# Mixing three weight tiles in every attention unit instead of three and two in turn, in a fused linear attention and spectral mixing kernel

## The chip, the cores and the metric

The kernel runs on one core of one Trainium2 chip. The metric is device time in microseconds (us) of one execution; kernels that are compared ran in turn on the same chip. Before the change, three runs took 444.5 to 444.66 us, with a median of 444.56. A *load* is a transfer from the chip's memory into a buffer, *in flight* from its issue to its landing. A ratio is the mean time of one kernel's fast runs over that of the other's fast runs of the same rounds, so it is not quite the ratio of the medians that are quoted.

## The reference, cut to what matters

```python
# 1. linear attention: batch 8, 8 heads, 576 tokens, 64 per head; phi makes 2 x 128 features
proj = x @ w_phi; proj -= max(abs(proj))
phi(x) = concat(exp(proj), exp(-proj))
num = phi(q) @ (phi(k).T @ v);  den = phi(q) . sum(phi(k)) + 1e-6
x = num / den                                     # -> (8, 576, 512)
# 2. spectral mixing: 64 modes, each with its own complex 512 x 512 matrix (128 MB in float32)
X = rfft(x, axis=1)
Y[:, m] = X[:, m] @ (w_r[m] + 1j * w_i[m])        # m < 64
u = x + irfft(Y)
out = u + relu(u @ w_ch)
```

## The kernel before

The matrices are loaded as 64 *weight tiles*: a tile is 8 modes x 128 input channels x 512, real or imaginary part. It is 1 MB in bf16 on the chip and is cast from 2 MB of float32 by the load. Attention runs in 16 *units* (two heads, two batches each), in a software pipeline. Four units make a channel group, and after a group's four units its 16 tiles can be *mixed*: 8 small matmuls per tile. Mixing a tile frees its buffer, and only then is the next load issued:

```python
pw_cm = tc.tile_pool(name="pw", bufs=8)      # weight tiles

def some(n):
    for _ in range(n):
        if mixq:
            key = mixq.pop(0)
            mix(*key, wts.pop(key), XTb[key[0] % 2], ...)
            if key not in held:
                next_w(1)                    # issue one more weight load, on POOL's queue

for n in range(-2, len(units) + 1):
    P, Q, K, R = (unit(n + i) for i in (-1, 0, 1, 2))
    X = 0 if n < 4 else 6 if n == 4 else 3 if n % 2 or n > 11 else 2
    # ... attention work of units n-1 .. n+2; loads of k, q, v two units ahead ...
    some(1 if X else 0)     # in the middle, twice
    # ...
    some(X - 2)             # at the end
```

Tiles that are still unmixed after attention are mixed in a second stage. There the time between mixes is filled with other TensorE work, the list `todo`. Its last 42 entries (`A`) need the sums of modes 0 to 47 for all channels, so they can only start after the 56th tile, the last tile of the fourth group that reaches them:

```python
todo += [c.only_x for c in ab[K:]] + [c.only_w for c in ab[K:]] + [c.all for c in ab[:K]]
A = 3 * 3 + K                                # K = 33
# ... def back(...) reads rows 0:96 of yall and zall, i.e. the 6 x 16 rows of o < 6
while mixq:                                  # the second stage
    # ... mix(...), next_w(1) ...
    n = -(-max(len(todo) - A, 0) // (left - 7)) if left > 7 else ...
    # ... fill(n)
```

The 8 tiles that remain after that (modes 48 to 63 of groups 2 and 3) are mixed among these 42 entries, and a tail writes the output.

Of the kernel before, what the change touches and what calls it, by code (L numbers as in the profile page):

```python
# [43 lines left out]
def kernel(  # L44
# [55 lines left out]
    class Unit:  # L100
# [43 lines left out]
        def rows(self, tT, i, out):  # L144
# [7 lines left out]
            else:  # L152
# [3 lines left out]
            src = ps.rearrange("p (a c) f -> p a c f", a=2) if len(out.shape) == 3 else ps  # L156
            dve.tensor_reduce(out=out, in_=src, axis=AX.X, op=ALU.max,
                              apply_absolute_value=True)
# [198 lines left out]
    def next_w(n):  # L357
        for _ in range(n):
            if wq:
                key = wq.pop(0)  # L360
                wts[key] = wload(*key)
# [65 lines left out]
    def forward_table():  # L427

        for p0, p1, d, n in ((0, 128, 0, 4), (0, 64, 4, 1), (64, 128, 5, 1)):
            src = csf[p0:p1, min(d, 4):min(d, 4) + n]  # L430
            dst = CF[p0:p1, d:d + n]
            for x in range(2):
                dve.tensor_scalar_mul(
                    out=dst[:, :, :, x, :], scalar1=1.0 - 2.0 * x,
                    in0=src[:, :, x, :].rearrange("p c (t m) -> p c t m", t=2))
        dve.tensor_scalar(out=mi[:, 0:1], in0=pi, scalar1=0, scalar2=1,
                          op0=ALU.logical_shift_right, op1=ALU.bitwise_and)
        dve.tensor_copy(mf[:, 0:1], mi[:, 0:1])
        for i in range(2):
            for n in range(4):  # L440
                sign, b = ((-1.0, 1.0), (1.0, 0.0))[n % 2]
                dve.tensor_scalar(out=side[:, i, n:n + 1], in0=mf[:, 0:1],
                                  scalar1=sign * (1.0 - 2.0 * i), scalar2=b * (1.0 - 2.0 * i),
                                  op0=ALU.mult, op1=ALU.add)
# [29 lines left out]
# [4 lines that stand above are left out]
                mix(*key, wts.pop(key), XTb[key[0] % 2], lambda: one([128, DMODEL]))  # L478
                if key not in held:
                    next_w(1)  # L480
# [6 lines left out]
    def unit(i):  # L487
        return units[i] if 0 <= i < len(units) else None

    for n in range(-2, len(units) + 1):  # L490
        P, Q, K, R = (unit(n + i) for i in (-1, 0, 1, 2))
        X = 0 if n < 4 else 6 if n == 4 else 3 if n % 2 or n > 11 else 2
        if Q:
            Q.exp_q(0)
        if K:
            K.rows_k(0)
            K.exp_k(0)
        if Q:
            Q.weigh_v2()
            if unit(n + 2):  # L500
                unit(n + 2).load_v()
        if P:
            P.freq()
            P.keep_x()
            if P.bp == NP - 1:
                mixq += [key for key in order if key[0] == P.g and (P.g < 2 or key[1] < 12)]
            if n == 4:
                some(2)
        if Q:
            Q.cols_q(1)  # L510
            Q.exp_q(1)
        some(1 if X else 0)
        if K:
            K.rows_k(1)
            K.exp_k(1)
        if Q:
            Q.kv()
        if K:
            K.rows_q(0)
            K.rows_k(2)  # L520
            K.rows_q(2)
            K.rows_q(1)
        if Q:
            Q.cols_q(2)
            Q.keep_kv()
            Q.exp_q(2)
        if K:
            K.exp_k(2)
            K.weigh_v()
        some(1 if X else 0)  # L530
        if K:
            K.shift_q()
        if Q:
            Q.num(0)
        if K:
            K.cols_q(0)
        if R:
            R.turn_k(0)
            R.turn_k(1)
            if unit(n + 4):  # L540
                unit(n + 4).load_k()
        if Q:
            Q.num(6)
        if R:
            R.turn_q(0)
            R.turn_q(1)
            if unit(n + 4):
                unit(n + 4).load_q()
        if Q:
            Q.num(12)  # L550
        some(X - 2)
        if n == -1:
            forward_table()
        if n < 3:
            next_w((2, 3, 2, 3, 2)[n + 2])
        if n == 6:
            pool.dma_start(wchb, moe_w_ch.rearrange("(dc p) e -> p dc e", p=128))
# [290 lines left out]
    while mixq:  # L848
# [13 lines left out]
        n = -(-max(len(todo) - A, 0) // (left - 7)) if left > 7 else math.ceil(len(todo) / (left - 0.4)) if left else 0  # L862
# [99 lines left out]
```

## Time and profile before

| | |
|---|---|
| three timed runs | 444.5 to 444.66 us |
| the execution that was profiled | 449.08 us, span 447.3 us |
| software DMA queue's packets | 99.1% of the span |
| TensorE matmuls busy | 76% |
| last weight tile landed | 410.45 us, its mix began at 410.49 |

These are lines of the page of the kernel before; a slice is a fortieth of the span, PEclk is the clock that TensorE was granted, in tenths.

```profile
span 447.3 us, 10461 instructions
...
PEclk9998897789988998958988889696999999999998
DMA  8999999999999999999999999999999999995697
GB/s 166 236 211 210 238 213 236 237 215 259 211 216 232 237 236 238 224 208 230 213 226 233 205 236 193 186 193 212 212 218 221 222 219 218 210 225 102 213 382 288
...
q0 software_dynamic: 45280, 86.19, 99.1%
```

The DMA engines look busy up to the 36th slice. Yet slices 25 to 27 move 186 to 193 GB/s where the ones after them move 212: a busy share does not tell a full queue from a thin one. The next lines are the windows view of the same run (stretch and length in us, each engine's busy time, then granted clock, DMA share and GB/s):

```profile
190.00:270.00 80.00, 61.89 (x992) 46.54 (x1000) 53.83 (x98) 55.92 (x99) 16.02 (x22) 0.84 1.12 221
270.00:300.00 30.00, 23.38 (x456) 17.61 (x459) 22.08 (x45) 16.36 (x30) 8.00 (x11) 0.89 1.09 188
```

In the timeline of POOL, which issues the weight loads, each line is start, duration, instruction and, in brackets, how long POOL was idle and what ended it:

```profile
263.97 0.74 POOL L37 DMA_DIRECT2D wt<-in_moe_w_r_dram  x1 [5.00 <-PE one L37]
270.06 0.74 POOL L37 DMA_DIRECT2D wt<-in_moe_w_i_dram  x1 [5.35 <-PE one L37]
273.28 0.74 POOL L37 DMA_DIRECT2D wt<-in_moe_w_r_dram  x1 [2.48 <-PE one L37]
280.55 0.74 POOL L37 DMA_DIRECT2D wt<-in_moe_w_i_dram  x1 [6.53 <-PE one L37]
287.21 0.74 POOL L37 DMA_DIRECT2D wt<-in_moe_w_r_dram  x1 [5.92 <-PE one L37]
```

Every load waited for TensorE (a mix) to free its buffer. The landings of these five, from the trace's semaphores, are 274.58, 279.88, 285.27, 290.75 and 298.14: 5.3 to 7.4 us apart, where a full queue gives 4.9 to 5.0. The Trainium skill, "Perfetto Trace Analysis" (section "Identifying Performance Opportunities"), says that the same gap repeating on the engine that should be saturated can mean that there is no memory for the next tile; here that is literally so.

Last, the chain of waits of the kernel before, near its end (start, duration, what):

```profile
338.41 33.88 DMA wt<-in_moe_w_r_dram
...
372.33 0.69 PE pt L37 x8
...
373.31 37.14 DMA wt<-in_moe_w_i_dram
...
410.49 0.66 PE pt L37 x8
```

It says that weight loads set the pace up to the last mix, at 410.49. And these are TensorE's waits for weight tiles between 363 and 412 us (us in total, times, longest):

```profile
PE pt L37 <- DMA wt<-in_moe_w_i_dram: 2.0, 2, 1.5
PE pt L37 <- DMA wt<-in_moe_w_r_dram: 0.4, 2, 0.2
```

### The profile page before, as it was taken

The page shows a single profiled execution, that of the slowest core. Times are in us where ns is not written, and L with a number is a line of the kernel's source. Part 1 is how long each engine was busy: PE and PEld are TensorE (multiplying, and loading weights), DVE is VectorE, ACT ScalarE, POOL GpSimd, SP SyncE. Part 2 cuts the span into 40 slices and gives each one's busy share as a digit, 9 for nine tenths or more (in the row PEclk, how much of TensorE's full clock was granted, in tenths as well). Part 3 has the DMA queues.
Part 4 walks back from the last instruction along what each step waited for, and adds up shares of the span by engine and source line. Part 5 has one row for each costly group of instructions (what it writes and reads, how often), then busy time and mean ns, then how long its engine had stood idle before and what let it go on. Part 6 is the DMA issues. An engine that isn't in the chain of part 4 may idle for free.

```text
span 447.3 us, 10461 instructions
## 1 busy us (share of the span) xinstructions
PE 339.9 (76%) x4389; PEld 219.4 (49%) x4433; DVE 283.9 (63%) x561; ACT 279.5 (62%) x488; POOL 84.4 (19%) x126
## 2 busy tenths in 40 slices
PE   2576677677686766787885787887799679999994
PEld 2355556545565555564664655652354344343231
DVE  4656685556765866748767668768743233775685
ACT  4596797666877975957877758434443232665673
POOL 7132132122211231221221111140102110000000
PEclk9998897789988998958988889696999999999998
DMA  8999999999999999999999999999999999995697
GB/s 166 236 211 210 238 213 236 237 215 259 211 216 232 237 236 238 224 208 230 213 226 233 205 236 193 186 193 212 212 218 221 222 219 218 210 225 102 213 382 288
DMA packets 51487, 99.31 MB, mean 222 GB/s; under 512 B 2480, under 2 KB 13616, under 8 KB 51440
## 3 DMA queue, kind: packets, MB, share of 16 engines
q0 software_dynamic: 45280, 86.19, 99.1%
q1 hardware_dynamic: 6160, 12.45, 7.9%
q8 instruction: 34, 0.56, 0.5%
q14 instruction: 13, 0.11, 0.1%
HBM read 163.64 MB, written 9.44 MB: 387 GB/s over the span
## 4 chain that ended last, share of the span: by engine, by line
issue 29%; PE 22%; DMA 20%; ACT 11%; DVE 10%; POOL 6%; POOLq 0%; ACTq 0%; DVEq 0%
DMA wt<-in_moe_w_r_dram 10%; DMA wt<-in_moe_w_i_dram 8%; PE pt L37 8%; PE one L37 7%; PE two L37 5%; ACT AB L37 4%; POOL wt L37 3%; DVE m L37 3%; ACT AQ L37 2%; DVE mk L37 2%; PE pp L37 2%; DMA qb<-in_q_dram 2%; DVE xw L37 1%; ACT XT L37 1%; ACT qT L37 1%
## 5 line engine op out<-in xcount | busy, mean ns | idle before, releaser
L37 ACT ACTIVATE AB<-two 128x1024 bf16<-128x1024 f32 x64 | 62.2, 1031 | 10.7 <-DVE mk L37 7.1
L37 ACT ACTIVATE AQ<-two 128x1024 bf16<-128x1024 f32 x64 | 62.7, 1046 | 3.6 <-PE two L37 3.4
L37 ACT CAST xw<-pt 128x512 bf16<-128x512 f32 x50 | 29.4, 587 | 44.6 <-PE pt L37 40.9
L37 DVE TENSOR_REDUCE mk<-two 128x8 f32<-128x1024 f32 x32 | 38.9, 1217 | 14.8 <-PE two L37 14.8
L37 DVE TENSOR_REDUCE m<-two 128x8 f32<-128x1024 f32 x32 | 39.1, 1223 | 13.9 <-PE two L37 13.8
L37 DVE RECIPROCAL rd<-one 128x6 f32<-128x6 f32 x48 | 9.4, 195 | 57.2 <-PE one L37 57.2
L37 PE MATMUL pt<-wchb,xT 128*128 128x512 bf16 x128 | 37.0, 405 | 8.3 <-DVE xT L37 6.3
L37 DVE TENSOR_TENSOR va<-vn,ee 128x1152 bf16<-128x1152 f32 x32 | 41.9, 1354 | 0.0
L37 ACT COPY kT<-one 128x512 bf16<-128x512 bf16 (+1 forms) x32 | 19.2, 640 | 32.5 <-PE one L37 32.4
L37 PEld LDWEIGHTS <-xs 128*128 128x128 bf16 x624 | 31.9, 104 | 14.2 <-issue 7.6
L37 PEld LDWEIGHTS <-minus 96*128 96x128 bf16 x288 | 28.8, 118 | 18.4 <-issue 13.8
L37 POOL DMA_DIRECT2D wt<-in_moe_w_r_dram x30 | 22.3, 744 | 75.1 <-PE one L37 42.9
L37 PE MATMUL two<-w2blk,qT 128*128 128x256 bf16 x128 | 21.0, 290 | 20.3 <-ACT AB L37 10.4
L37 PE MATMUL two<-mT,minus 96*128 96x128 bf16 x256 | 31.9, 261 | 4.0 <-issue 3.0
L37 POOL DMA_DIRECT2D wt<-in_moe_w_i_dram x28 | 20.9, 746 | 69.4 <-PE one L37 34.9
L37 PEld LDWEIGHTS <-qT 128*128 128x128 bf16 x144 | 14.3, 102 | 36.2 <-issue 33.5
L37 PE MATMUL one<-kvz,AQ 128*128 128x65 bf16 x512 | 29.6, 217 | 0.0
L37 PE MATMUL one<-wt,XT 128*32 128x512 bf16 x288 | 24.9, 435 | 4.4 <-DVE XT L37 2.7
L37 PEld LDWEIGHTS <-XT 128*32 128x32 bf16 x512 | 15.0, 149 | 26.7 <-issue 13.6
L37 DVE TENSOR_TENSOR xs<-one,rd 128x384 bf16<-128x384 f32 x48 | 26.7, 557 | 1.6
L37 POOL DMA_DIRECT2D kb<-in_k_dram x16 | 11.5, 717 | 85.2 <-PE one L37 84.4
L37 PEld LDWEIGHTS <-AQ 128*128 128x128 bf16 x512 | 26.4, 115 | 1.4 <-issue 0.4
(132 smaller groups left out, 699.3 us busy)
## 6 DMA issues: line engine op xcount, KB each, us to landing
wt<-in_moe_w_r_dram POOLq DMA_DIRECT2D x30, 1024.0 KB, 20.7
wt<-in_moe_w_i_dram POOLq DMA_DIRECT2D x28, 1024.0 KB, 19.6
vn<-in_v_dram POOLq DMA_DIRECT2D x15, 576.0 KB, 12.3
out_dram<-of SPq DMA_DIRECT2D x16, 512.0 KB, 3.0
kb<-in_k_dram POOLq DMA_DIRECT2D x16, 288.0 KB, 12.3
qb<-in_q_dram POOLq DMA_DIRECT2D x16, 288.0 KB, 12.7
xs<-in_moe_w_i_dram POOLq DMA_DIRECT2D x2, 1024.0 KB, 23.6
yacc<-in_moe_w_r_dram POOLq DMA_DIRECT2D x1, 1024.0 KB, 9.6
```

Source lines behind the costliest of these rows:

```text
L37: ins = f(*args, **kwargs)
```

## The change

The intent is to issue weight loads earlier, so that the queue does not run thin. The whole diff:

```diff
-        X = 0 if n < 4 else 6 if n == 4 else 3 if n % 2 or n > 11 else 2
+        X = 0 if n < 4 else 6 if n == 4 else 3
```

Indices 6, 8 and 10 mix a third tile. At index 7 the first group runs out one tile sooner, so the net gain is one tile from the end of index 8 and two from the end of index 10: 43 tiles instead of 41 are mixed during attention. No work is added or removed.

## The prediction

> **What bounds the kernel now.** The DMA engines: busy 90% or more in nearly every slice of the page, the software queue's packets taking 99% of the span. The chain of waits ends in weight loads, the last issued at 373.3 us and landed at 410.45; its mix began at 410.49, and a 36 us tail follows. In a deep queue landings follow each other by 4.9 to 5.0 us for a weight tile and 1.4 to 1.5 for q, k, v. The list of waits shows no attention instruction waiting for a DMA.
>
> **Where it loses.** Between 187 and 298 us loads are issued only when a mix frees a buffer, with two or three in flight; issue to landing takes about 10 us, against over 20 earlier. Landings then follow by 5.3 to 5.9 us, once 7.4, and the windows from 270 to 300 us move about 185 GB/s, against 212 at depth. Over 190 to 300 us this loses about 7.6 us (an estimate from those spacings), against 1.2 in 110 to 190. The Trainium skill, "DMA: Bandwidth & Descriptors" (section "Anatomy of one DMA"), gives a DMA a fixed cost of about 2 us, mostly completion latency; the trace agrees in that it shows only when few are queued.
>
> **What the change does.** It adds and removes no work. Units 6, 8 and 10 each mix a third tile; group 0 then runs out one tile earlier in unit 7, so the net is one tile ahead from the end of unit 8 (180 us) and two from unit 10 (215). 43 tiles instead of 41 are mixed in attention, 21 instead of 23 later. Each early mix issues a load early, so the queue is one, then two deeper where it runs dry. The tiles are there: mixes in units 8 to 14 start 30 to 49 us after their tile landed.
>
> Cost: a mix is 0.66 us of PE (up to 1.08 at a lowered clock). Two more lengthen attention by about 1.5 us; the later stage loses the same. The k, q, v loads queue behind 5 to 10 us more of weights, but are issued about 34 us before use.
>
> **On the critical path.** Recovering about 6 of the 7.6 us brings the last landing to about 404.5. PE must keep up: after attention it runs 4 to 11 us behind the landings until 340, then waits for tiles, 7.4 us in all from 345 to 410.5, but only about 1 us after 378. So it can follow by about 7 us at best, less what the coarser spread of filler work costs. I take 5 us.
>
> **Prediction.** 439.5 us, 8 in 10 between 436.8 and 443.3. Faster by over 2%: 0.05; within 2%: 0.94; slower: 0.01.
>
> **What would show the steps right.** From 215 to 300 us weight landings 4.9 to 5.0 us apart, four or more loads in flight, over 205 GB/s from 270 to 300; the last landing at 403 to 406; attention ending within 2 us of before; a tail of 35 to 36 us; PE's gaps for weight tiles from 345 to 410 shrunk to about 2 us.
>
> **What would make it wrong.** If the slow spacing comes from contention with the engines, the landing stays near 410, the time near 444. If PE is limited between 300 and 345 us by dependences rather than work, mixes lag their tiles, buffers come free late, and the gain shrinks to 1 to 3 us. If attention lengthens by 4 us or more, it is lost.

## The result, and the profile after

| | before | after |
|---|---|---|
| median of 4 runs, us | 444.53 | 444.77 |
| lowest to highest | 444.0 to 444.66 | 443.93 to 445.16 |
| execution that was profiled | 449.08, span 447.3 | 444.49, span 442.4 |

The ratio is 1.0005, with a 95% interval of 0.9988 to 1.0023: the same, where 439.5 us was predicted. Yet the two *profiles* differ by 4.9 us, nearly the 5 us of the prediction. Lines of the page of the kernel after:

```profile
span 442.4 us, 10508 instructions
...
PEclk9789888688989988988888789698899998999998
DMA  7999999999999999999999999999999999993697
GB/s 166 237 211 210 238 212 236 238 212 264 211 213 236 239 236 235 213 239 211 238 219 230 234 215 238 212 212 213 212 224 222 219 219 219 212 224 78 216 383 286
```

The dip of slices 25 to 27 is gone (238, 212, 212). Its windows view and POOL's timeline:

```profile
190.00:270.00 80.00, 62.93 (x1027) 47.05 (x1024) 54.03 (x96) 56.32 (x98) 17.17 (x24) 0.85 1.13 228
270.00:300.00 30.00, 22.27 (x421) 15.77 (x419) 20.32 (x45) 14.86 (x28) 7.41 (x10) 0.87 1.12 215
```

```profile
262.07 0.74 POOL L37 DMA_DIRECT2D wt<-in_moe_w_r_dram  x1 [4.99 <-PE one L37]
267.90 0.74 POOL L37 DMA_DIRECT2D wt<-in_moe_w_i_dram  x1 [5.09 <-PE one L37]
271.12 0.74 POOL L37 DMA_DIRECT2D wt<-in_moe_w_r_dram  x1 [2.48 <-PE one L37]
278.40 0.74 POOL L37 DMA_DIRECT2D wt<-in_moe_w_i_dram  x1 [6.54 <-PE one L37]
```

POOL still waits for mixes just as long, but each of these loads is two tiles further down the list: four or five loads, the new one included, are now in flight at each issue between 250 and 290 us, where two or three were. Landings of weight tiles that follow each other directly are 4.9 to 5.0 us apart there, once 5.3. The chain of waits after:

```profile
329.81 31.91 DMA wt<-in_moe_w_i_dram
...
361.76 0.68 PE pt L37 x8
...
363.76 5.82 PE pt L37 x36
...
405.65 0.59 PE pt L37 x6
```

The load that ends in it at 361.7 is that of the 56th tile. After it no weight load appears in the chain; it is TensorE to the end. TensorE's waits for weight tiles from 340 to 363 us are

```profile
PE pt L37 <- DMA wt<-in_moe_w_i_dram: 4.7, 2, 3.2
PE pt L37 <- DMA wt<-in_moe_w_r_dram: 0.9, 1, 0.9
```

and from 363 to 412 us the list has none.

So nearly everything about the queue went as foreseen in the two traces, and the timed runs did not move. The profiled execution of before took 449.08 us, 1% more than any of its timed runs.

### The profile page after: what moved, and what is told of

The parts are those of the page before. It is cut to its first block, busy times and chain, and to the rows that moved or that the text cites. A ratio compares the mean times of both kernels' runs of the same rounds, so it can differ in the third digit from the quotient of the medians.

```text
span 442.4 us, 10508 instructions
## 1 busy us (share of the span) xinstructions
PE 340.6 (77%) x4433; PEld 215.7 (49%) x4433; DVE 284.4 (64%) x561; ACT 279.4 (63%) x488; POOL 84.7 (19%) x126
## 4 chain that ended last, share of the span: by engine, by line
issue 33%; DMA 30%; PE 17%; POOL 7%; ACT 6%; DVE 4%; POOLq 0%; ACTq 0%; DVEq 0%
DMA wt<-in_moe_w_i_dram 17%; PE pt L37 8%; DMA vn<-in_v_dram 6%; PE pp L37 5%; DMA wt<-in_moe_w_r_dram 5%; POOL wt L37 4%; PE two L37 3%; ACT AB L37 2%; ACT AQ L37 2%; DMA qb<-in_q_dram 2%; DVE m L37 1%; PE one L37 1%; POOL kb L37 1%; DVE mk L37 1%; POOL qb L37 1%
## 5 line engine op out<-in xcount | busy, mean ns | idle before, releaser
L37 PE MATMUL pt<-wchb,xT 128*128 128x512 bf16 x136 | 37.9, 405 | 5.4 <-DVE xT L37 4.1
L37 PE MATMUL two<-qT,w2blk 128*128 128x512 bf16 x64 | 30.8, 481 | 4.6 <-ACT AQ L37 4.4
L37 PE MATMUL one<-wt,XT 128*32 128x512 bf16 x304 | 27.1, 444 | 6.6 <-DVE XT L37 2.7
L37 PE MATMUL two<-mT,minus 96*128 96x128 bf16 x256 | 31.0, 256 | 0.0
```

The costliest lines, as they stand in the source:

```text
L37: ins = f(*args, **kwargs)
```

## The experiments

Two quantities read from each trace are used below. The *loss* is the sum, over the landings of POOL's loads between 190 and 300 us, of their spacing less 4.93 us for a weight tile and 1.43 us for k, q or v (the spacings of a full queue in the trace of before). The *56th tile* is the one that opens the last 42 filler entries. "The pace" is the start of ScalarE's last `ee` instruction, in the last attention unit.

### 1. The two kernels again, and an emptier queue

No edit for the first two. The third is

```diff
-        X = 0 if n < 4 else 6 if n == 4 else 3 if n % 2 or n > 11 else 2
+        X = 0 if n < 4 else 6 if n == 4 else 2
```

> The kernel before, unchanged. The profile of before was of an execution of 449.08 us, 1% over its three timed runs (444.5 to 444.66). Theory S (sample): that execution was not a typical one; a new profile has a span of about 442.5 us, the last weight landing near 405, and under 3 us lost in the spacing of landings from 190 to 300 us. Theory G (given back): every execution of before loses about 7 us there, the last landing is near 410, and the new profile has a tail or a later stage that is some 5 us shorter than in the profile of the kernel after. A span of 447 again would say that profiles of before are longer than its timed runs.

> The changed kernel, unchanged. Both theories: 444 to 445 us, span about 442.5, under 2 us lost in the spacing of landings from 190 to 300 us, last landing near 405, as in its first profile. If its last landing moves by 4 us or more between two profiles, single profiles of this kernel can't be compared at this level.

> Two tiles in every unit from the fifth on, so 32 tiles instead of 41 are mixed in attention, and loads are issued later by up to nine tiles. If an emptier queue costs DMA time (both theories), the queue holds one or no load at a time from about 190 us on, it idles for 20 us or more before 300 us, and the time is over 460 us. If the queue is not what bounds this stretch, the time stays within 5 us of before.

Before took 445.33 to 446.84 us (profiled: 446.84), after 444.82 to 446.11 (profiled: 445.49). Seven further runs of before on that chip took 444.98 to 452.08, the highest of them counted as slow. The ratio of the changed kernel to these seven was 0.9931 (0.9847 to 1.0016); that of the kernel before, run once more beside them, was 0.9943 (0.9872 to 1.0014). So this ratio says nothing of the change: the same program gives it too. The new profile of before lay between the two theories: loss 5.7 us, last landing 407.98, span 445.1. The new one of after repeated the first: loss 2.04 (under 2 was expected), last landing 405.06; its highest time, 446.11, is also above the 444 to 445 that was expected.

Two tiles in every unit took 477.46 us (ratio 1.065). Its loss was 28.5 us from 190 to 300 us and 8.3 more before that. The 56th tile landed at 395.5 us instead of 365.3, and the time grew by as much, 30 us. The idle queue of 20 us or more that was expected did not come: between 190 and 300 us it held no load for 3 us and at most one for 46. Most of the loss came with a load under way: one that was issued with none in flight still took 7.9 us to land, where a full queue lands one every 4.9 to 5.0. So a thin queue does cost time, one for one; how thin it gets in the kernel before differs from one execution to the next.

### 2. What sets the end: the last tiles, or TensorE?

These kernels load half of the bytes of some tiles and use that half twice. Their outputs are wrong, which doesn't matter for the times. For the last 8 tiles the condition is `g >= 2 and o >= 6`, for tiles 45 to 56 it is `g == 3 and o < 6`:

```diff
+        if g >= 2 and o >= 6:
+            pool.dma_start(wt[:, :, 0], w[...].rearrange("m (p r) e -> p m r e", r=2)[:, :, 0])
+            return wt
...
-                    rhs=wt[:, j, r, :], ...
+                    rhs=wt[:, j, 0 if g >= 2 and o >= 6 else r, :], ...
```

> The changed kernel; the last 8 weight tiles (from the 57th on) load only half of their bytes, so the result is wrong on purpose. Theory P (TensorE): once the 56th tile is mixed, the remaining work on TensorE alone takes about 43 us to the last mix and 37 more to the end (80.4, 79.8, 80.6 and 81.8 us in the four profiles so far), whenever the last tiles land. Then the time stays within 1.5 us of the changed kernel's 445. Theory D (DMA): the last landing sets the end; 8 tiles at about 2.1 us less each bring it up to 17 us earlier, and the time falls by over 6 us.

> The kernel before with half of the bytes in the last 8 tiles (wrong on purpose). My prediction had the last landing bound the kernel. Theory P: from the 56th tile on TensorE is the limit before the change too, so the time is within 1.5 us of before's, with the last mixes 5 us or more behind their landings. Theory D: the time falls by over 4 us.

> The changed kernel; tiles 45 to 56 load only half of their bytes, wrong on purpose. Theory P: the mix of the 56th tile can move earlier only by the gaps in which TensorE waits for tiles before it, 4.4 to 5.6 us in the two profiles of the changed kernel, so the time is 439 to 442 us. Theory D: these landings come up to 25 us earlier and the time falls by over 10 us. No change at all would say that not even this landing matters.

| kernel | median, us | its fast runs | TensorE, from the traces |
|---|---|---|---|
| last 8 halved, after | 444.96 | 444.49, 444.56, 445.35 | profile slow (468.54), not used |
| last 8 halved, before | 445.34 | 444.49 to 445.5 | last tile landed at 383.47, mixed at 406.90 |
| tiles 45 to 56 halved, after | 439.92 | 439.06 to 440.48 | 56th tile landed at 335.58, mixed at 356.60 |

With the last tile landing over 20 us before its use, the kernel before still took 445.3 us (before in the same rounds: 445.5). The last landings bound neither kernel; that the last tile landed at 410.45 and was mixed at 410.49 was a coincidence of two nearly equal paths: with no tile halved, the last mix began 0.04 to 2.7 us after the last landing in every trace, slow or fast. Halving the 12 tiles up to the 56th, in the changed kernel, gained 5 us (439.92, against 444.96 with the last 8 halved in the same rounds) and no more, which is about what TensorE waits for the last three of these tiles (4.7 + 0.9 us, the wait for the 56th itself included). With those gone its waits from 300 to 362 us start, in this trace, with

```profile
PE pt L37 <- DVE xT L37: 4.2, 4, 2.1
PE pt L37 <- ACT xw L37: 1.8, 6, 0.5
```

and contain no load. So the end is set thus: *the 56th tile lands, and from there about 80 us of TensorE work and tail follow.* In the table at the end of this section that remainder is 79.8 to 81.9 us in all twelve traces. It counts from the landing only where TensorE waits for that tile. In the trace with tiles 45 to 56 halved, which the table leaves out, it is 100.8 us from the landing and 79.8 from the mix.

### 3. Attention made slower

```diff
+        if 5 <= n < 16:
+            junk = one([128, 512])
+            for _ in range(3):
+                pe.matmul(junk, lhsT=ident_b, start=True, stop=True, rhs=...)   # 128x512, unused
         some(X - 2)
```

> The kernel before with three unused 128x512 matmuls at the end of each of units 5 to 15, an estimate of 7 us of TensorE in all. Theory W (pace): before, loads leave only at the pace of attention's mixes and the queue is nearly empty from 190 us on, so slower attention is passed on to the landings. The loss in the spacing from 190 to 300 us grows by 3 us or more, and the 56th tile lands 3 to 7 us later than in the new profile of before (365.3); time 448 to 453. Rival: the spread of before's time has nothing to do with the pace of attention; the landings and the time stay within 2 us.

> The same matmuls in the changed kernel. Theory W: the deeper queue covers the slower attention; the 56th tile lands within 1.5 us of 361.8, and the time grows by 0 to 3 us, at least 2 us less than that of before does. Rival: both kernels grow by the same.

Before took 452.44, 453.83, 457.4 and 456.82 us (mean 455.1); it took 447.3 in the mean of the same rounds without the extra work. After took 445.9, 450.18 and 447.36 us (mean 447.8), and 454.05 in an execution counted as slow. With slower attention the change is thus worth 7 us (5.7 with the execution of 454.05 counted, whose granted clock of 0.886 is hardly lower than the 0.888 of the one of 450.18), and theory W's difference of at least 2 us is there; the ratios to before in these rounds, 1.0167 (1.0097 to 1.0236) and 1.0003 (0.9931 to 1.0076), have intervals that do not overlap. The size for before (8 us) is above what was expected (at most 453 us), and its loss grew from 5.7 to only 7.9 us by 300 us, less than the 3 us said, with 3.8 us more between 300 and 328; its 56th tile did land 5.2 us later, as said. One more part missed: the only profile of the slowed kernel after is that slow execution, in which its queue ran thin too (two to five loads in flight, loss 6.1 us) and the 56th tile landed at 371.67. So the deeper queue covers some lateness, not any amount. (The unused slow trace of the changed kernel with the last 8 tiles halved lies between: pace 289.3, loss 3.7 us, 56th tile at 363.7.)

### 4. Attention made faster

The 18 matmuls of each unit that subtract q's row maximum are left out from the seventh unit on (wrong):

```diff
+            self.lean = NP * g + bp > 5
...
         def shifted(self, out, n, stop):
+            if self.lean:
+                return
```

(The `stop` flag of the matmul before them becomes `stop=self.lean`.)

> The kernel before without the 18 shift matmuls of each unit from the seventh on (wrong on purpose), so that attention is faster. Theory W: the mixes come sooner, the queue of before no longer runs dry, the loss in spacing from 190 to 300 us falls from 5.7 to under 3 us, the 56th tile lands at 361 to 363, and the time is 442 to 445 with a spread under 2 us. Rival: the loss belongs to the shallow queue alone and stays at 5 to 8 us, the 56th tile at 364 or later.

> The same omission in the changed kernel. Theory W: its queue was deep already, so the 56th tile lands at 361 to 362 as before and the time is 442 to 445, within 1.5 us of the faster-attention version of before: the change is worth nothing when attention is fast, where it was worth 7 us when attention was slowed. Rival: it keeps a lead of 2 us or more.

Before took 444.51 to 446.94 us (mean 446.0), after 444.14 to 446.1 (mean 444.8). The difference of the means, 1.2 us, is inside the 1.5 that theory W allowed, and the loss of before was 2.9 us, under 3. But its times spread by 2.4 us, not under 2, its median of 446.22 is above 445, and its 56th tile landed at 363.1, just outside. The omission did not make attention fast reliably. This pair leans towards W without settling it.

### 5. More runs of both

> The changed kernel once more, in five rounds, for the size of the difference. Theory W (pace): its times spread by about 2 us (444 to 446 so far), those of before by more (444 to 452 so far), because only before hands attention's pace on to the DMA queue; so the ratio is between 0.99 and 1.00, and the lowest times of the two agree within 1 us. Rival (no effect): the ratio's interval holds 1 and both spread alike.

> The kernel before once more, for a third profile and more times. Theory W with P: whatever its time, the 56th tile lands 79 to 81.5 us before the end of the profiled span, and the loss in spacing from 190 to 300 us goes with the pace of attention: if the profiled execution takes 445 us or less, the loss is under 4 us and the 56th tile lands at 361 to 363.5; if it takes 447 or more, the loss is over 5 us and the tile lands at 365 or later. The times again lie between 444 and 452 us, with a spread wider than the changed kernel's 2 us. A fast execution with a loss of 6 us, or a slow one with a loss of 2, would refute it.

The changed kernel took 444.1 to 445.61 us in six runs. Eleven runs of before on that chip took 443.92 to 450.02, and the ratio was 0.9967 (0.992 to 1.0013). The interval holds 1, as the rival said. The spread differs, as W said, but this is no proof of W: it compares six runs of the kernel under test with the eleven that were taken of before beside all kernels (its *standing* runs). On another chip, the kernel before itself took 443.96 to 445.36 us in its six runs, a spread of 1.4 us where over 2 was expected, beside eleven standing runs of 444.29 to 449.47 us of the same program (ratio 0.9979, 0.9938 to 1.002). The third profile of before, of the execution of 443.96 us, has the loss, the landing and the remainder that W and P foretold. Its windows view:

```profile
190.00:270.00 80.00, 61.09 (x1127) 45.51 (x1127) 59.77 (x105) 61.09 (x107) 17.55 (x24) 0.96 1.12 227
270.00:300.00 30.00, 23.04 (x363) 15.33 (x362) 21.88 (x78) 12.50 (x26) 7.39 (x10) 0.89 1.12 210
```

and its chain of waits:

```profile
329.65 32.08 DMA wt<-in_moe_w_i_dram
...
361.77 0.69 PE pt L37 x8
...
363.77 5.57 PE pt L37 x36
```

Same kernel, same program as the first profile: 210 GB/s instead of 188 from 270 to 300 us, three or four loads in flight instead of two or three, a loss of 2.4 us instead of 7.6. The chain is that of the kernel *after*: the 56th tile's load to 361.7 us, and TensorE from there. From 190 to 270 us TensorE was granted 0.96 of its clock here and 0.84 in the first profile, and 1127 instead of 992 matmuls ran in that window. A kernel before in a fast execution has next to nothing left for the change to recover (a loss of 2.4 us, against 1.7 to 2.0 in the three traces of after).

All traces together, in the order of the pace within each kind (us):

```
trace                      profiled   pace    loss   56th tile  end less that
before, last 8 halved      445.50    272.9    2.3    362.7      81.0
before, third              443.96    274.7    2.4    361.7      80.5
before, faster attention   446.61    275.5    2.9    363.1      81.7
before, again              446.84    280.4    5.7    365.3      79.8
before, first              449.08    280.8    7.6    366.9      80.4
before, slower attention   452.44    284.5    7.9    370.5      80.2
two in every unit          477.88    280.7   28.5    395.5      80.5
after, faster attention    444.14    275.7    2.4    361.7      80.6
after, first               444.49    278.7    1.7    361.7      80.7
after, in five rounds      445.55    279.9    1.7    362.3      81.4
after, again               445.49    280.9    2.0    361.9      81.9
after, slower (slow state) 454.05    295.3    6.1    371.7      80.5
```

Read the middle columns. In the kernel before, the loss and the 56th landing roughly follow the pace of attention. In the kernel after they do not, up to a pace of 281; at the same pace of about 280 to 281 the tile lands at 361.9 to 362.3 instead of 365.3 to 366.9.

## Why the prediction was wrong

**What put the number off is one step: "I take 5 us", taken off the median of the timed runs.** The loss of 7.6 us was read in an execution of 449.08 us and subtracted from executions of 444.56 us, which had hardly had it. (They were not traced themselves; the traced one of 443.96 us lost 2.4.) Taken off the execution that it was read in, the same gain gives 449.08 - 5 = 444.1 us; the measured median is 444.77. The span of 447.3 us looked close enough to 444.56 to hide this, but a span here is about 1.8 us shorter than the time of the same execution (449.08 and 447.3; 443.96 and 442.2), so the timed runs had spans of about 442.8. Over all runs, 50 fast executions of the kernel before took 443.9 to 451.5 us, with a median of 445.4, and 18 of them took over 446.2; 14 of the changed kernel took 443.9 to 446.1, with a median of 445.1. (These are pooled; the ratios quoted above are the ones to trust for size, and none of them is clear of 1 for the two kernels themselves.) The best times are the same. Whether the change cuts the slow tail is not shown: of the ten runs in which the kernel before was itself the kernel under test (experiments 1 and 5), one took over 446.2 us (446.84), against none of 14; of the other 17, 16 are among the standing runs of before and one is its first profile. Why the standing runs spread more is open. That the four runs of before next to the first result were all good ones (444.0 to 444.66) is chance or a property of that chip; this stays open.

Point by point:

- **"What bounds the kernel now: the DMA engines", to 410.45 us.** Right up to the 56th tile, wrong after it. From there TensorE is the limit, in both kernels: halving the last 8 loads changed nothing (445.3 and 445.0 us). The chain of waits named loads to the end because the two paths are nearly equal in every trace with whole tiles (0.04 to 2.7 us apart at the last mix), and in that one TensorE waited a moment for three of these loads. That TensorE waited less than 1 us for those loads was the warning.
- **"Where it loses": 7.6 us with two or three loads in flight.** Right for that execution, and the cause is right: two tiles in every unit made it 28.5 us. Not right for the kernel: 2.4 us in a fast execution.
- **What the change does to the queue.** Right: four or five in flight, landings 4.9 to 5.0 us apart from 215 us on where one weight tile follows another, but for one of 5.3, 215 GB/s from 270 to 300 us, last landing at 405.15 (403 to 406 was said), tail 36.9 us (35 to 36 was said, but it was 36.8 before too), attention not lengthened (pace 278.7 against 280.8).
- **"PE's gaps for weight tiles shrunk to about 2 us".** Wrong: 5.6 us remained. They lie at the 54th to the 56th tile. The filler that can run without the 56th tile is a fixed amount (34 of the 76 entries of `todo`, dealt out two or three to a tile), and the rest needs that tile. An earlier landing moves these gaps; it does not fill them. Instead the waits after that tile went to nothing.
- **"It can follow by about 7 us at best".** This bound came from the sum of the gaps. What counts is when the 56th tile lands: 366.9 us in the first profile of before, 361.7 in that of after. That is 5.2 us, and the spans differ by 4.9. That the 5 us came out right for these two traces is therefore partly luck: it was worked out from a bound that did not apply.
- **"If attention lengthens by 4 us or more, it is lost"** did not come up: the change did not lengthen it. Attention that is slow for another reason is where the change helps: 7 us with the extra matmuls.

What makes one execution's attention slower than another's was not isolated. The granted clock goes with it (0.84 and 0.85 from 190 to 270 us in the two slower profiles of before, 0.96 in the fast one and in that with the last 8 tiles halved), and the Trainium skill, "TensorE: Matmul & The Clock Gate" (section "Part 1: The HAM clock gate"), describes a clock that idleness lowers, judged in free-running windows, and calls its effect run-variable. But the kernel after ran at 0.85 there too and its queue stayed full, and a lower clock may follow from a TensorE that waits as well as cause it. That the pace, whatever sets it, reaches the DMA queue in one kernel and, up to a pace of 281 us, not in the other is what the runs show.

## What to carry to other kernels

Compare the time of the profiled execution with the timed runs before pricing a bubble: what one trace loses can only be taken off the execution that lost it, and a second profile is cheap. Where loads are issued as buffers come free, a queue that is one or two tiles deeper pays where the work that frees the buffers runs late (7 us with attention slowed on purpose) and leaves the best time as it was. Run the unchanged kernel once more as if it were the changed one: here its ratio of 0.9943 told how little 0.9931 meant. Last, a chain of waits that ends in a load proves little when the engine behind it hardly waits for it: halve the load's bytes and see whether the end moves.

## What the Trainium skill lacked or had wrong

- "DMA: Bandwidth & Descriptors" (section "Anatomy of one DMA") gives a fixed cost of about 2 us for each DMA, but not how many must be in flight to hide it. Here weight loads of 1 MB landed 4.9 to 5.0 us apart in the kernel after between 278 and 322 us, with four or more in flight at issue, and 5.3 to 7.4 us apart in the first profile of before, with two or three.
- The same page (section "Bandwidth") lists 341 GB/s for 1 MB and 425 for 16 MB, measured with one core busy and without a case that casts, and says in "Where 436 GB/s comes from" that the HBM side binds at about 358 GB/s. Here a tile of 1 MB written from 2 MB read took 4.93 us in a full queue: 212 GB/s written, and twice that, about 425, read (an estimate from the spacing); the page of the first profile counts 387 GB/s of HBM traffic over the whole span. Both are above the 358, so for this one core it is no limit; the page's own 425 says the same.
- "TensorE: Matmul & The Clock Gate" (section "Part 1: The HAM clock gate") puts the ramp at the start under 1% of a typical span and describes clock drops after idle gaps, but has no figure for how far the clock of one program differs between executions in mid-kernel. Here, in one program, the granted clock from 190 to 270 us was 0.84 in one execution and 0.96 in another, and their times were 449.08 and 443.96 us, 1.2% apart. The runs do not show how much of that the clock caused.
- "Perfetto Trace Analysis" has nothing on whether the traced execution is a typical one. Here the first trace was of 449.08 us beside timed runs of 444.5 to 444.66.
